# Attention and two MoE layers in one kernel: three units of the first stage transposed by VectorE and moved by GpSimd's queue, and the fourth chunk's bias written a group at a time

## The chip, the cores and the metric

One core of a Trainium2 chip runs one program. The metric is device time in microseconds (us), the median of several executions. The engines are TensorE (PE in the profile, its weight loads PEld), VectorE (DVE), ScalarE (ACT), GpSimd (POOL) and SyncE (SP, which here only issues transfers). A transfer is issued by a queue (SP's, GpSimd's, ScalarE's) and carried by the same 16 DMA engines.

## The reference

Attention with a bias that depends on the distance of the two positions, then two feed-forward layers (their weights are float64, the rest float32), for 4 sequences of 576 tokens, 8 heads of 64:

```python
x = (np.log1p(np.abs(rel)) / psi_i)[..., None]
h = np.maximum(x @ w1 + b1, 0.0)            # 32 hidden values
bias = h @ w2                               # one per head
scores = scale * np.matmul(q, k.transpose(0, 1, 3, 2)) + bias.transpose(2, 0, 1)[None]
attn = softmax(scores); out = np.matmul(attn, v)
x = attention output as 2304 tokens x 512
y = (sigmoid(x @ w_gate) * (x @ w_val)) @ w_out          # 512 -> 1536 -> 512
h = y @ w_in                                             # 512 -> 2048
out = (h * np.clip(h + 3, 0, 6) / 6) @ w_out2            # 2048 -> 512
```

## The kernel before, in words

The 576 query positions are cut into five chunks (`QC`, line 25), four of 128 and one of 64. The work goes in stages: a first stage computes the attention of chunk 0, and then block k (k = 0 to 4, `block`, line 833) computes the feed-forward layers of chunk k in 68 steps of 12 matmuls (`moe_step`, line 592; `product`, line 565), with the attention of chunk k+1 put in between. TensorE executes its instructions in the order in which they are written. In the first stage all engines but GpSimd keep the written order (`manual_schedule`, line 648), in block 0 TensorE and SP, later TensorE alone; the rest is ordered by the tile framework's scheduler.

**The first stage** (lines 645 to 703) handles 16 units. A unit is one sequence and a pair of heads, 128 queries by 2 x 576 keys. After the bias of the first chunk and of four groups of the second, the loop over n (line 679) has these parts in iteration n:

- `att_load` (281): SP's loads of unit n+3. The pools hold 6 buffers of k and 7 of v.
- `att_exp` (330), ScalarE: the exponentials of unit n.
- `att_min` (315), VectorE: unit n+1's scores plus bias, with their minimum (of the negated scores). It frees the PSUM buffers into which `att_qk` writes next.
- `att_tr` (351): unit n-1's nine 128x128 transposes on TensorE, in three parts, each copied by ScalarE from PSUM into `pT`.
- `att_norm` (339), VectorE: unit n divided by its sums.
- `att_av` (390), TensorE: the products with V of unit n-2, and `att_x` (410): their high half on ScalarE (424) and low half on VectorE (425).
- `att_qk` (299), TensorE: unit n+2's products of q and k. They need both PSUM buffers of `s1`, so unit n+1's minimum first.
- `w_part` (509), VectorE: one sixth of the conversion of one of the first two weight blocks from packed doubles into a high and a low half; block 0 on iterations 4 to 9, block 1 on 10 to 15. The sixth part also issues the store of the converted block on SP's queue (533).

From block 0 on, weights are loaded with `w_load` (495), converted with `w_split` (536, first use of each block) and, from block 1 on, read back converted.

**Later chunks.** Chunk 1 is transposed as above. Chunks 2 to 4 are handled by pairs of units (`chunk_pairs`, 765): `pair_qk` (428), `pair_soft` (473), whose `att_turn` (368) lets VectorE transpose each 32x32 block (line 373), and `pair_turn` (378), which moves the blocks to their partitions with 16 transfers (line 383), on GpSimd's queue, for chunks 2 and 3 half of them on SP's. The products with V (`pair_av`, 486) follow `lag` steps after the start of the pair.

**The bias.** A group G is 16 query positions. `bias_hidden` (136) makes the hidden values of a quarter of a group, on ScalarE or VectorE; `bias_mm` (153) multiplies them with w2 on TensorE; for chunks 1 to 3 the bias is symmetric, and `bias_out2` (177) writes two groups at once, the right part on ScalarE, the mirrored left part on VectorE, into a tile, and issues two transfers to DRAM. With `apart` it takes each group's result from a buffer of `m1` (four one-bank PSUM buffers, line 77, which the matmuls of the steps, of the transposes, of `pair_qk`'s tails and of the products with V use too) rather than from `s1` (two buffers of two banks, line 76, which hold the scores). `cv_t` (95) holds a constant per partition, which replaces a term for the quarters that VectorE makes.

**Order and due times.** `block_events` (809) gives each piece of attention work a due step; `block` carries out what is due before each step's 12 matmuls. For block 1 (k = 1): chunk 2's bias from step 2, pairs of chunk 2 at 21 + 5.11 i, chunk 3's bias at (line 820)

```python
ev += chunk_bias(3, 23.2 + 1.5 * d, d / 2)
```

with d = 46/9 = 5.11 steps. In block 3 the last chunk's four pairs start 18.8 steps apart, from 0.5, and the products with V come 10 steps after a start, the last at step 67 (line 828). Steps 24 to 35 and 46 to 53 of a block are the output products, in which an open sum stays in one buffer of `m1` for three or two steps.

## Time and profile before

| | us |
|---|---|
| median of 3 runs | 1108.26 |
| lowest and highest of them | 1106.01, 1110.21 |
| the profiled execution | 1106.79 |
| its span in the profile | 1105.0 |

| engine | share of the span in which it is busy |
|---|---|
| TensorE matmuls | 99% |
| TensorE weight loads (beside them) | 80% |
| VectorE | 60% |
| ScalarE | 47% |
| GpSimd | 12% |

The span reaches from the first to the last instruction of the profiled execution; 1.79 us of its time lie around it. Busy time of TensorE is modelled at its end, as its matmuls overlap; whether it stands still is read from its waits. The profile's lines give an instruction as line, engine, operation, output <- inputs by the names in the program. "Idle before" is the engine's time without work just ahead of an instruction, with what ended it. The chain of waits follows back, from the last instruction, what each one waited for.

### The profile page before, as it was taken

To read this page: it belongs to the slowest core of one execution; us is meant where nothing else is said; L and a number is where in the kernel's file an instruction comes from. 1 tells how busy PE (TensorE), PEld (TensorE's weight loads), DVE (VectorE), ACT (ScalarE), POOL (GpSimd) and SP (SyncE) were. 2 spreads that over 40 slices of the span, in tenths; PEclk is the share of its full clock that TensorE was granted. 3 is DMA by queue.
4 is the path that set the end of the run, shared out by engine and by line. 5 is a ranking of instruction groups with operands and counts; after the bars stand their busy time and mean duration, and the time that the engine had idled before them with its cause. 6 is when DMAs were issued, how large, how long until landed. Compare 5 with 4: busy or idle time off the path is not lost.

```text
span 1105.0 us, 19878 instructions
## 1 busy us (share of the span) xinstructions
PE 1094.5 (99%) x7142; PEld 884.0 (80%) x7142; DVE 668.0 (60%) x1529; ACT 524.7 (47%) x1052; POOL 129.7 (12%) x248
## 2 busy tenths in 40 slices
PE   8999999999999999999999999999999999999998
PEld 4777777777777788777888878788788787879998
DVE  7999998898963456897725654656252417052232
ACT  7887686798863433565414342534032214121132
POOL 1000000000010002112221111111430202031000
PEclk9999999999999999999999999999999999999999
DMA  6958999999987688999988888798896978778997
GB/s 228 369 182 296 373 396 373 386 322 375 384 292 233 219 264 281 283 311 294 342 296 249 292 245 278 250 281 244 283 274 239 266 247 255 227 215 310 363 365 270
DMA packets 118769, 321.97 MB, mean 291 GB/s; under 512 B 21008, under 2 KB 29712, under 8 KB 118672
## 3 DMA queue, kind: packets, MB, share of 16 engines
q1 hardware_dynamic: 108000, 297.15, 79.0%
q0 software_dynamic: 9152, 23.21, 7.5%
q8 instruction: 57, 0.93, 0.3%
q10 hardware_dynamic: 1520, 0.35, 0.1%
q14 instruction: 40, 0.33, 0.1%
HBM read 245.09 MB, written 51.37 MB: 268 GB/s over the span
## 4 chain that ended last, share of the span: by engine, by line
PE 80%; DVE 7%; DMA 5%; ACT 4%; issue 3%; POOL 1%; ACTq 0%; DVEq 0%; POOLq 0%
PE ps L574 63%; PE ps L404 7%; PE ps L309 3%; PE ps L446 3%; PE ps L360 2%; DMA pT<-t 2%; PE ps L162 1%; PE ps L170 1%; DVE cm L546 1%; DMA wsp<-wp 1%; DVE cm L549 1%; DVE wp L555 1%; POOL outT L635 1%; ACT cm L544 1%; DVE s L324 1%
## 5 line engine op out<-in xcount | busy, mean ns | idle before, releaser
L574 PE MATMUL ps<-xyh,wp 128*128 128x512 f32 (+1 forms) x1600 | 468.1, 372 | 0.3
L574 PEld LDWEIGHTS ps<-xyh,wp 128*128 128x128 f32 x1600 | 290.5, 189 | 61.3 <-issue 4.9
L574 PE MATMUL ps<-gh,wp 128*128 128x512 f32 (+1 forms) x1120 | 330.2, 373 | 0.0
L574 PE MATMUL ps<-xyl,wp 128*128 128x512 f32 (+1 forms) x800 | 295.6, 370 | 0.4 <-DVE xyl L587 0.3
L574 PEld LDWEIGHTS ps<-gh,wp 128*128 128x128 f32 x1120 | 203.5, 189 | 37.8 <-issue 3.6
L574 PE MATMUL ps<-gl,wp 128*128 128x512 f32 (+1 forms) x560 | 206.9, 369 | 0.0
L574 PEld LDWEIGHTS ps<-xyl,wp 128*128 128x128 f32 x800 | 151.1, 189 | 24.6 <-DVE xyl L587 0.8
L383 POOL DMA_DIRECT2D pT<-t x192 | 94.3, 499 | 504.1 <-DVE t L373 136.3
L583 ACT ACTIVATE gh<-tmp 128x512 fp32r<-128x512 f32 (+1 forms) x140 | 82.2, 588 | 145.9 <-DVE tmp L605 103.3
L334 ACT ACTIVATE s<-s,m 128x576 f32<-128x576 f32 x144 | 110.4, 768 | 20.1 <-DVE m L468 14.4
L574 PEld LDWEIGHTS ps<-gl,wp 128*128 128x128 f32 x560 | 105.8, 189 | 16.8 <-DVE gl L585 0.6
L585 DVE TENSOR_TENSOR gl<-tmp,gh 128x512 fp32r<-128x512 f32 (+1 forms) x140 | 88.6, 634 | 47.3 <-ACT gh L583 46.4
L605 DVE SCALAR_TENSOR_TENSOR tmp<-tmp,ps 128x512 f32<-128x512 f32 (+1 forms) x60 | 37.8, 630 | 94.1 <-PE ps L574 92.7
L404 PEld LDWEIGHTS ps<-pT,vt 128*64 128x64 f32 x1600 | 79.4, 137 | 18.1 <-issue 12.6
L404 PE MATMUL ps<-pT,vt 128*64 128x128 f32 (+1 forms) x1600 | 92.4, 266 | 1.5 <-DMA pT<-t 0.9
L611 DVE SCALAR_TENSOR_TENSOR tmp<-tmp,ps 128x512 f32<-128x512 f32 (+1 forms) x80 | 50.0, 628 | 57.1 <-ACT tmp L610 55.5
L424 ACT ACTIVATE xyh<-ps 128x128 fp32r<-128x128 f32 (+1 forms) x52 | 16.5, 317 | 107.3 <-PE ps L404 107.1
L610 ACT ACTIVATE tmp<-ps 128x512 f32<-128x512 f32 (+1 forms) x80 | 43.9, 549 | 41.9 <-PE ps L574 40.4
L425 DVE TENSOR_TENSOR xyl<-ps,xyh 128x128 fp32r<-128x128 f32 (+1 forms) x52 | 17.7, 341 | 72.4 <-ACT xyh L424 72.1
L601 ACT ACTIVATE tmp<-ps 128x512 f32<-128x512 f32 (+1 forms) x60 | 33.1, 552 | 56.9 <-PE ps L574 56.9
L635 POOL DMA_DIRECT2D outT<-acc x40 | 27.7, 736 | 262.3 <-DVE acc L626 245.1
L147 ACT ACTIVATE z<-tz_t,zc_t,sc_t 128x576 f32<-128x576 f32 (+7 forms) x70 | 49.7, 766 | 13.2 <-PE ps L162 11.3
(73 smaller groups left out, 1096.5 us busy)
## 6 DMA issues: line engine op xcount, KB each, us to landing
wp<-wsp SPq DMA_DIRECT2D x272, 512.0 KB, 5.2
wd<-wpack SPq DMA_DIRECT2D x68, 512.0 KB, 6.7
wsp<-wp SPq DMA_DIRECT2D x68, 512.0 KB, 6.2
vt<-vd SPq DMA_DIRECT2D x80, 320.0 KB, 5.2
kt<-kd SPq DMA_DIRECT2D x80, 288.0 KB, 5.1
pT<-t POOLq DMA_DIRECT2D x192, 72.0 KB, 5.3
pT<-t SPq DMA_DIRECT2D x128, 72.0 KB, 5.0
bm<-biasD SPq DMA_DIRECT2D x15, 576.0 KB, 5.9
```

What stands on the lines that cost most here:

```text
L147: nc.scalar.activation(out=z, in_=x, func=AF.Relu, scale=sc_t[:, t:t + 1], bias=b1c)
L309: nc.tensor.matmul(out=ps[h][n * a:n * a + n, j, 0:NI], lhsT=qt[r, b + a, 0:n], rhs=kt[r, NI * j:NI * j + NI], start=True, stop=True, tile ...
L334: nc.scalar.activation(out=s[:, h], in_=s[:, h], func=AF.Exp, scale=-1.0, bias=d["m"][:, h:h + 1], accum_out=r[:, h:h + 1],)
L383: (nc.sync if p[0][0] < 4 and i > 1 else nc.gpsimd).dma_start(out=pt[32 * q:32 * q + 32, i].rearrange("j u t i -> j (u t i)"), in_=t[32 * ...
L404: nc.tensor.matmul(out=po[64 * h:64 * h + 64, n * a:n * a + n], lhsT=vt[:, v], rhs=pt[:, m * a:m * a + m, k, :], start=(t == 0), stop=(t = ...
L574: nc.tensor.matmul(out=ps[:, 0:nt], lhsT=w[:, c, :], rhs=x[:, 0:nt], start=(first and c == 0 and i == 0), stop=(last and c == 3 and i == 2),)
L583: nc.scalar.activation(out=hi[:, 0:nt], in_=src, func=AF.Copy, scale=scale)
L585: nc.vector.tensor_tensor(out=lo[:, 0:nt], in0=src, in1=hi[:, 0:nt].bitcast(F32), op=ALU.subtract)
L605: nc.vector.scalar_tensor_tensor(out=th, in0=th, scalar=1.0, in1=ps, op0=ALU.add, op1=ALU.mult)
L610: nc.scalar.activation(out=t, in_=ps, func=AF.Relu, bias=3.0)
L611: nc.vector.scalar_tensor_tensor(out=t, in0=t, scalar=6.0, in1=ps, op0=ALU.min, op1=ALU.mult)
L635: q.dma_start(out=out[2 * ih + x, o, :, :, lo - ih * NI:hi - ih * NI], in_=av[:, 2 * x:2 * x + 2, lo - i0:hi - i0],)
```

## The change

In the first stage three of the 16 units (numbers 2, 6 and 10) are no longer transposed by TensorE. VectorE transposes the 32x32 blocks of such a unit in one instruction, right after its scaling, into a tile with one buffer, and GpSimd's queue moves the blocks with 16 transfers of 36 KB into another tile, with two buffers. The products with V of such a unit come in iteration n+5 instead of n+2, ahead of the usual ones of that iteration. v has ten buffers instead of seven. The parts of the two weight conversions fall on other iterations (`CONV`). The two second-chunk groups that are written apart get a constant of their own, `cv1_t`, with one more quarter's product.

In the second block the fourth chunk's bias is made by groups: each group's hidden values half a pair's distance ahead of a pair's start, its products and its writing (`bias_out1`, SP's queue) just before that start, in one-bank buffers. In the fourth block the products with V of the last chunk's first three pairs come 11.5 steps after a start instead of 10.

```diff
--- before.py
+++ after.py
@@ -93,6 +93,7 @@
     sc_t = const.tile([128, S // 4], F32, name="sc_t")
     zc_t = const.tile([128, 3], F32, name="zc_t")
     cv_t = const.tile([128, 1], F32, name="cv_t")
+    cv1_t = const.tile([128, 1], F32, name="cv1_t")
     wm_t = const.tile([128, 1], F32, name="wm_t")
     w2b_t = const.tile([128, 32], F32, name="w2b_t")
     id_t = const.tile([128, 128], F32, name="id_t")
@@ -112,12 +113,13 @@
     nc.vector.tensor_scalar(out=sc_t, in0=sc_t, scalar1=zc_t[:, 0:1], scalar2=None, op0=ALU.mult)
     nc.vector.tensor_scalar(out=zc_t[:, 2:3], in0=b1c, scalar1=-1.0, scalar2=None, op0=ALU.mult)
     ps = mm_ps()
-    for g in (2, 3):
+    for g in (1, 2, 3):
         nc.tensor.matmul(
             out=ps[32 * g:32 * g + 32, 0:2], lhsT=w2b_t, rhs=zc_t[:, 0:2], start=True, stop=True,
             tile_position=(0, 32 * g),
         )
     nc.vector.tensor_scalar(out=cv_t[64:128], in0=ps[64:128, 1:2], scalar1=D ** 0.5, scalar2=None, op0=ALU.mult)
+    cps = ps
 
 
 
@@ -184,12 +186,12 @@
         if apart:
             for x, p in enumerate((ps, bo_q.pop(G + 1))):
                 nc.scalar.activation(
-                    out=bo[:, x, left:SU], in_=p[:, 0:right + 1], func=AF.Identity, scale=D ** 0.5, bias=cv_t
+                    out=bo[:, x, left:SU], in_=p[:, 0:right + 1], func=AF.Identity, scale=D ** 0.5, bias=cv1_t
                 )
             for x, p in enumerate((ps, p)):
                 nc.vector.tensor_scalar(
                     out=bo[:, x, 0:left], in0=p[:, left:0:-1],
-                    scalar1=D ** 0.5, scalar2=cv_t, op0=ALU.mult, op1=ALU.add,
+                    scalar1=D ** 0.5, scalar2=cv1_t, op0=ALU.mult, op1=ALU.add,
                 )
         else:
             nc.scalar.activation(
@@ -212,6 +214,26 @@
             (nc.gpsimd if c == 1 else nc.sync).dma_start(
                 out=rows[16 * x:16 * x + 16], in_=bo[:, x, 0:SU],
             )
+
+    def bias_out1(G):
+
+        ps = bo_q.pop(G)
+        c, x = 16 * G // NQ, G % 2
+        i0 = 16 * (G - x) - QC[c][0]
+        left, right, _ = reach(G)
+        if x == 0:
+            bo_t[1] = A["bo"].tile([128, 2, SU + 1], F32, name="bo")
+        bo = bo_t[1][:, x]
+        nc.scalar.activation(
+            out=bo[:, left:SU], in_=ps[:, 0:right + 1], func=AF.Identity, scale=D ** 0.5, bias=cv_t
+        )
+        nc.vector.tensor_scalar(
+            out=bo[:, 0:left], in0=ps[:, left:0:-1],
+            scalar1=D ** 0.5, scalar2=cv_t, op0=ALU.mult, op1=ALU.add,
+        )
+        at = NQ - 32 - i0
+        rows = biasD[c].rearrange("(h r w) -> r h w", h=H, w=SW)[i0 + 16 * x:i0 + 16 * x + 16, :, at:at + SU]
+        nc.sync.dma_start(out=rows, in_=bo[:, 0:SU])
 
     def bias_out(G, x=0, last=True):
 
@@ -365,6 +387,20 @@
             in_=ps[:, 0:3 * NQ].rearrange("p (t n) -> p t n", t=3), func=AF.Copy,
         )
 
+    def unit_turn(u):
+
+        t = A["t"].tile([128, 4, 9, 32], F32, name="t")
+        pt = st[u]["pt"] = A["pu"].tile([128, 4, 9, 32], F32, name="pT")
+        nc.vector.transpose(
+            out=t, in_=st[u]["s"].rearrange("p h j -> p (h j)").rearrange("p (t q j) -> p q t j", q=4, j=32)
+        )
+        for i in range(4):
+            for q in range(4):
+                nc.gpsimd.dma_start(
+                    out=pt[32 * q:32 * q + 32, i].rearrange("j t i -> j (t i)"),
+                    in_=t[32 * i:32 * i + 32, q].rearrange("j t i -> j (t i)"),
+                )
+
     def att_turn(p, x):
 
         u = p[x]
@@ -392,7 +428,7 @@
         n = QC[c][1]
         d = st[u]
         vts, pt = kv_q.pop(u)[1], d["pt"]
-        if c < 2:
+        if c < 2 and u not in TURNED:
             pt = pt.rearrange("j t (p i) -> j p t i", i=32)
         m = n // 32
         po = d["po"] = o_ps()
@@ -642,8 +678,11 @@
     us = units[0]
     NL = len(us)
     NG0, NG1 = QC[0][1] // 16, 2
+    TURN = (2, 6, 10)
+    TURNED = [us[n] for n in TURN]
+    CONV = (5, 7, 9, 11, 13, 14, 15, 15, 15, 16, 16, 17)
     with ExitStack() as lead:
-        for name, bufs in (("pt", 2), ("s", 3), ("k", 6), ("v", 7), ("bo", 3), ("wf", 2), ("cv", 2)):
+        for name, bufs in (("pt", 2), ("s", 3), ("k", 6), ("v", 10), ("t", 1), ("pu", 2), ("bo", 3), ("wf", 2), ("cv", 2)):
             A[name] = lead.enter_context(tc.tile_pool(name=name + "l", bufs=bufs))
         lead.enter_context(tc.manual_schedule(engines={ET.PE, ET.Activation, ET.DVE, ET.SP}))
         load_rows(us[0], False)
@@ -670,6 +709,8 @@
         for G in range(NG0 + NG1, NG0 + NG1 + 2):
             for g in range(4):
                 bias_hidden(G, g, 1)
+        nc.vector.tensor_scalar(out=cv1_t, in0=cv_t, scalar1=1.0, scalar2=None, op0=ALU.mult)
+        nc.vector.tensor_scalar(out=cv1_t[32:64], in0=cps[32:64, 1:2], scalar1=D ** 0.5, scalar2=None, op0=ALU.mult)
         att_qk(us[0])
         for G in range(NG0 + NG1, NG0 + NG1 + 2):
             bias_mm(G, True)
@@ -685,18 +726,22 @@
                 att_exp(us[n])
             if n + 1 < NL:
                 att_min(us[n + 1])
-            if 1 <= n <= NL:
+            if 1 <= n <= NL and n - 1 not in TURN:
                 for part in range(3):
                     att_tr(us[n - 1], part, mm_ps)
             if n < NL:
                 att_norm(us[n])
-            if n >= 2:
-                att_av(us[n - 2], mm_ps)
-                att_x(us[n - 2])
+            if n in TURN:
+                unit_turn(us[n])
+            for m in (n - 5, n - 2):
+                if m >= 0 and (m in TURN) == (m == n - 5):
+                    att_av(us[m], mm_ps)
+                    att_x(us[m])
             if n + 2 < NL:
                 att_qk(us[n + 2])
-            if 4 <= n < 16:
-                w_part((n - 4) // 6, (n - 4) % 6)
+            for part in range(12):
+                if CONV[part] == n:
+                    w_part(part // 6, part % 6)
             if n == NL - 4:
                 gate = issued[0]
             if n == NL:
@@ -817,7 +862,10 @@
             d = (last - 21.0) / 9
             ev += chunk_bias(2, 2.0, 1.5)
             ev += chunk_pairs(2, 21.0, d, 2 * d, last)
-            ev += chunk_bias(3, 23.2 + 1.5 * d, d / 2)
+            for g in range(8):
+                a = 21.0 + d * (g + 1)
+                ev.append((a - d / 2, lambda G=24 + g: [bias_hidden(G, t) for t in range(4)]))
+                ev.append((a - 0.005, lambda G=24 + g: (bias_mm(G, True), bias_out1(G))))
         elif k == 2:
             d = (last - 9.5 - 0.5) / 7
             n4 = 2 * S - 4 - 4 * 16 * 8
@@ -825,7 +873,7 @@
             ev += chunk_pairs(3, 0.5, d, d, last)
             ev += chunk_bias(4, d + 2.7, d)
         elif k == 3:
-            ev += chunk_pairs(4, 0.5, (last - 10.5) / 3, 10.0, last)
+            ev += chunk_pairs(4, 0.5, (last - 10.5) / 3, 11.5, last)
         return [e[::2] for e in sorted((e[0], n, e[1]) for n, e in enumerate(ev))]
 
     held = []
```

## Rows read from the trace of the kernel before

**Rows 1.** The page: busy time by engine; chain that ended last, by engine.

```profile
PE 1094.5 (99%) x7142; PEld 884.0 (80%) x7142; DVE 668.0 (60%) x1529; ACT 524.7 (47%) x1052; POOL 129.7 (12%) x248
...
PE 80%; DVE 7%; DMA 5%; ACT 4%; issue 3%; POOL 1%; ACTq 0%; DVEq 0%; POOLq 0%
```

**Rows 2.** What TensorE waited for, whole kernel: us in total, times, longest us.

```profile
PE ps L404 <- DMA pT<-t: 0.9, 1, 0.9
...
PE ps L360 <- DVE s L347: 0.4, 1, 0.4
```

**Rows 3.** Chain of waits in the first stage: start us, us, what.

```profile
43.09 1.17 PE ps L309 x8
44.26 1.14 PE ps L360 x9
45.40 1.24 PE ps L404 x20
...
81.50 1.17 PE ps L360 x9
...
88.48 11.63 PE ps L574 x50
```

**Rows 4.** Busy us by stretch, first stage: length, engines (instructions), PEclk, DMA share, GB/s.

```profile
35.93:50.12 14.19, 14.19 (x151) 10.91 (x149) 12.24 (x39) 11.82 (x32) 0.00 (x0) 1.00 1.04 389
...
sum 42.65, PE 42.63 PEld 32.71 DVE 39.51 ACT 35.46 POOL 0.00; mean PE 14.21 PEld 10.90 DVE 13.17 ACT 11.82 POOL 0.00
```

**Rows 5.** VectorE's timeline, first stage: start us, us, instruction, idle before it.

```profile
37.20 0.76 DVE L324 CUSTOM_DVE_ANT_0 s<-ps,bm 128x576 f32<-128x576 f32 x1 [0.55 <-PE ps L309]
...
40.75 0.76 DVE L324 CUSTOM_DVE_ANT_0 s<-ps,bm 128x576 f32<-128x576 f32 x1 [0.55 <-PE ps L309]
...
42.11 0.16 DVE L341 TENSOR_SCALAR r<-r 128x2 f32<-128x2 f32 x1
...
43.45 0.29 DVE L425 TENSOR_TENSOR xyl<-ps,xyh 128x128 fp32r<-128x128 f32 x1
43.66 0.43 DVE L518 TENSOR_SCALAR cm<-wd 128x512 f32<-128x512 f32 x1
...
47.84 0.76 DVE L324 CUSTOM_DVE_ANT_0 s<-ps,bm 128x576 f32<-128x576 f32 x1 [0.22 <-PE ps L309]
...
50.75 0.68 DVE L522 SCALAR_TENSOR_TENSOR cm<-wd,cm 128x512 uint32<-128x512 uint32 x1
51.39 0.76 DVE L324 CUSTOM_DVE_ANT_0 s<-ps,bm 128x576 f32<-128x576 f32 x1
```

**Rows 6.** VectorE's timeline, second block, a transposition.

```profile
410.06 1.38 DVE L373 STREAM_TRANSPOSE t<-s 128x1152 f32<-128x1152 f32 x1
```

**Rows 7.** GpSimd's timeline, its transfers of transposed pairs.

```profile
412.07 3.95 POOL L383 DMA_DIRECT2D pT<-t  x8 [72.57 <-issue]
...
638.17 4.03 POOL L383 DMA_DIRECT2D pT<-t  x8 [20.65 <-DMA wp<-wsp]
...
869.00 4.03 POOL L383 DMA_DIRECT2D pT<-t  x8 [45.87 <-DVE t L373]
...
877.17 2.44 POOL L383 DMA_DIRECT2D pT<-t  x5 [1.38 <-DMA pT<-t]
```

**Rows 8.** DMA issues, 20 to 36 us: KB each, median us to landing.

```profile
bm<-bo SPq DMA_DIRECT2D x2, 36.0 KB, 2.3
```

**Rows 9.** DMA issues by line, 868.5 to 886 us.

```profile
pT<-t POOLq DMA_DIRECT2D x16, 72.0 KB, 6.0
```

**Rows 10.** Tile pT, 412 to 424 us: landing of its transfers.

```profile
DMA to landing us min/median/max: 3.2/3.8/4.5
```

**Rows 11.** SP's timeline, first stage: issue of the first block's store.

```profile
62.10 0.33 SPq L533 DMA_DIRECT2D wsp<-wp  x1
```

**Rows 12.** VectorE's timeline, first block's start and third block.

```profile
88.47 1.29 DVE L555 TENSOR_TENSOR wp<-cm,wp 128x512 fp32r<-128x512 f32 x2
...
638.12 2.03 DVE L149 TENSOR_SCALAR z<-tz_t,sc_t,zc_t 128x576 f32<-128x576 f32 x4
```

## The prediction

> **What bounds the kernel now.** I read the page's busy line and its chain first: TensorE is busy for 1094.5 of 1105.0 us, and the chain that ended last is 80% TensorE [rows 1]. Then the list of what TensorE waited for: nine waits in the whole kernel, none above 1.1 us; two that matter below are in [rows 2]. So no stage has idle time to win back. The kernel gets shorter only by work that leaves TensorE or by one of these waits, and longer by every new one.
>
> In the first stage (to 84 us) the chain goes in iterations of one unit: products of q and k 1.17 us, nine transposes 1.14, products with V 1.24, together 3.55 [rows 3]. The busy times of its steady part show that VectorE is nearly as full: 39.5 of 42.65 us, TensorE 42.63, at a granted clock of 1.00, the 2.4 GHz level [rows 4]. VectorE's timeline gives one iteration: the minimum 1.36 us (40.75 to 42.11), the scaling 1.34 (to 43.45), the low half of an output 0.21 (to 43.66). That is 2.91, and then one part of a weight conversion, 0.43 long or 0.64 to the next start (50.75 to 51.39). An iteration with the long part, 47.84 to 51.39, takes 3.55 us and has no gap [rows 5]. VectorE's room is thus 0.64 us in an iteration without a part, and nothing in one with a long part.
>
> **The change, part by part.**
>
> *Off TensorE and ScalarE:* three times nine transposes, 3 x 1.14 = 3.4 us of TensorE; and nine copies on ScalarE, which has room (35.5 of 42.65 us [rows 4]) and so gives nothing.
>
> *Onto VectorE:* three transpositions of 128x1152; one of that shape takes 1.38 us [rows 6]. The parts of the conversions move to make room: one on each of iterations 5, 7, 9, 11, 13 and 14, six on 15 to 17.
>
> *What VectorE then can do, iteration by iteration.* Before, the minimum of unit 4 starts at 37.20 after 0.55 us of waiting [rows 5]. The first transposition, 1.38, comes ahead of it: 0.83 later, 38.0. Iterations 3 to 5 take 2.91, 2.70 (no products with V, so no low half) and 2.91 + 0.43: the minimum of unit 7 starts at 46.95, before at 47.84. Iterations 6 to 9 take 2.91 + 1.38, 2.91 + 0.21 + 0.43, 2.70, and 2.91 + 0.64: 14.1 us, where the kernel before took 4 x 3.55 = 14.2 and TensorE alone would need 14.2 - 1.14 = 13.1. Iterations 10 to 13 come to 14.1 again. So unit 15's minimum starts at 75.15, some 1.05 us earlier than before (47.84 + 8 x 3.55 = 76.2), and not 3.4. VectorE sets the pace, and TensorE stands for a few tenths at a time.
>
> *The tail gives that back.* With its last q·k product done at about 75.3, TensorE has two groups of transposes and two products with V ahead of unit 15's transposes, and now also unit 10's product, which is five behind: 2 x 1.14 + 3 x 1.24 = 6.0, and some 0.3 for the scaling of unit 14: 81.6, against 81.50 [rows 3]. I put the first stage at **0.0**; its ends are -2.6 (the second rival) and late data (the first).
>
> *Will the data be there?* Behind each transposition sixteen transfers of 36 KB go out from GpSimd's queue, in which nothing stands in that stretch (0.00 us busy [rows 4]). Eight issues take 3.95 us [rows 7], sixteen 7.9 to 8.2. No row shows such a transfer from this queue. Its landing lies between 2.3 us, a 36 KB transfer from SP's queue [rows 8], and 6.0, this pattern with 72 KB in a full stretch [rows 9]; there the queue also stood for earlier landings, so that sixteen issues took from 869.00 to 879.61, 10.6 us [rows 7]. From the end of a transposition to the last landing that makes 7.9 + 2.3 = 10.2 to 10.6 + 6.0 = 16.6 us. I take 12.0: 8.2 and the 3.8 of a 72 KB stretch in which the queue never stood [rows 10], because half the bytes weigh against the fuller DMA here. The first to wait is VectorE itself, as the transposed tile has one buffer. The first transposition ends at about 37.7 (the low half that waited for nothing but its product, 0.29, then 0.55 of idle, move behind it), the second is due at 46.95 + 2.70 = 49.6, so 11.9 us are there: just in time, no cost, no margin.
>
> *SP's queue.* The store of the first converted block stood in it until 62.10 [rows 11], waiting for the sixth part, with the loads of units 13 to 15 behind it. It now follows all the loads, and V has ten buffers for seven: loads only get earlier. They also fill a stretch that was nearly free of transfers while unit 6's transfers run, which speaks for the first rival.
>
> *The six late parts* (3 x 0.43 + 3 x 0.64 = 3.2 us) delay VectorE's conversion of the third weight block. It is ready at 88.47 + 0.7 = 89.2 [rows 12]. The 50 products from 88.48 on [rows 3] are two that end the first step and four steps of 2.8 us, so the third step starts at 91.7. VectorE's three transpositions and these parts are 1 to 2.5 us there: no cost, up to 0.5.
>
> *Start.* One more product of two columns, two VectorE instructions of one column, long before anything waits for them: no cost, up to 0.2.
>
> *Fourth chunk's bias a group at a time* (second block). The same products and the same eight transfers; eight narrower evictions of each kind for four wide ones. No wait of TensorE lies there, so nothing is won. But the results now take a buffer of the pool of four: at steps 32 and 47 an open sum holds one, and the pair's second tail needs the one of the products with V just ahead. If VectorE is in a transposition then, TensorE stands 1.38 us at most; the bias products between give it more than that time. No cost, up to 1.4 at each of two places.
>
> *Last chunk's products with V 1.5 steps later.* One wait was there, 0.9 us [rows 2]; a step of 2.8 us is now between. **-0.9**, with 0 as the other end if the transfers are later too.
>
> Sum: 0.0 + 0.0 - 0.9. The profiled execution took 1106.79 us, 1.79 more than its span; so 1105.9. The median of the three runs shown is 1.47 above that execution: **1107.4 us**.
>
> **A rule weighed.** While VectorE ran four scalings, 2.03 us from 638.12 [rows 12], eight issues of GpSimd took 4.03 us, against 3.95 without [rows 7]. *The Trainium skill, "SBUF — State Buffer", section "Who interferes with whom", says that a VectorE instruction in a two-port mode, into which scalings can go, and GpSimd shut each other out for the whole instruction; by that the eight issues would have taken up to 2 us longer, and this row does not show it.* I keep 3.95; the other outcome is the third rival.
>
> **Rivals.**
>
> *Data late (slower).* With 16.6 us, the second transposition stands 16.6 - 11.9 = 4.7 us on VectorE, and behind it every minimum for which TensorE's next q·k product waits. The third has 14.1 - 1.4 = 12.7 us, so 0 to 3.9 more. It decides from about 12 us on. For it: transfers at 1.04 of the DMA's share in 35.93 to 50.12 [rows 4], and earlier loads. Against: half the bytes. Middle price 6: 1113.4 us. Chance 0.18.
>
> *VectorE keeps up (faster).* By totals VectorE needs 39.5 + 4.1 - 3.2 = 40.4 us in the steady part and TensorE 42.6 - 3.4 = 39.2, so at least 1.2 of the 3.4 is lost; with the wait of 0.4 before unit 15's transposes [rows 2] gone, -2.6. For it: these totals; against: the order inside each four iterations. 1107.4 - 2.6 = 1104.8. Chance 0.14.
>
> *Issues stop while VectorE scales.* Two scalings are at most 1.3 us of each 3.55 (the 1.34 above). Sixteen issues would take 7.9 x 3.55 / 2.25 = 12.5, the data is there after 16.3, 4.4 late, then 3.6: 1107.4 + 8 = 1115.4. Chance 0.04.
>
> *Buffers of the second block* decide: 1.4 twice, 1110.2. Chance 0.06.
>
> **How the numbers follow.** My forecast has 0.58; its own range, with the spread of the three runs (1106.0 to 1110.2), is 1105.5 to 1109.5. Half a per cent, about what a measurement of this kernel can tell from no change, is 5.5 us: below 1102.7 or above 1113.8. The first needs the second rival and luck: 0.04. The second needs the dearer half of the late data, or the third rival: 0.11. Between them 0.85. The range 1104.0 to 1113.0 takes in the second and fourth rival and the cheaper half of the first; it leaves out some 0.04 below and 0.13 above.
>
> **What would show it.** Right: 13 groups of nine transposes for 16 in the first stage; VectorE without gaps from 37 to 75 us and TensorE waiting there for a minimum or a scaling; unit 15's transposes still near 81.5; no wait for the three units' transfers, and none at the last chunk. Wrong: products with V (line 404) or VectorE's transposition waiting for a transfer (late data); unit 15's transposes before 79.5 (VectorE keeps up); waits of TensorE in the second block (buffers).

## The result, and the profile after

The changed kernel takes 1117.06 us (median of 6 runs, 1115.99 to 1121.29), the kernel before 1106.82 in the same series: a ratio of 1.0093, 95% interval 1.0078 to 1.0107 (the ratios here and below are taken from the executions, not from the two medians, and so are not always their quotient). It is slower, and outside the range. The span of the profiled execution is 1114.8 us, 9.8 more than before.

The page of the changed kernel, busy time by engine and the chain that ended last, against [rows 1]:

```profile
PE 1095.8 (98%) x7117; PEld 882.8 (79%) x7117; DVE 672.3 (60%) x1538; ACT 522.9 (47%) x1047; POOL 154.8 (14%) x296
...
PE 89%; DMA 4%; DVE 3%; ACT 1%; issue 1%; POOL 1%; SPq 0%; ACTq 0%; DVEq 0%
```

TensorE is busy as long as before (1095.8 against 1094.5 us). The 9.8 us are therefore mostly waits. The chain does not say which: transfers of `pT` have 2% of it before and after. TensorE's list of waits does (us in total, times, longest), against [rows 2]:

```profile
PE ps L440 <- DMA pT<-t: 6.7, 2, 3.5
PE ps L610 <- DVE wp L591: 1.5, 3, 0.7
```

The first line is new, and it alone is 6.7 us. TensorE's timeline (start us, us, instruction, idle before it) has its two places, the products with V of units 2 and 6, each in one row with those of an ordinary unit, hence x40. The third row, with unit 10's, waits for nothing. The last four rows I use further below:

```profile
54.22 2.40 PE L440 MATMUL ps<-pT,vt 128*64 128x128 f32 x40 [3.52 <-DMA pT<-t]
...
72.07 3.79 PE L440 MATMUL ps<-pT,vt 128*64 128x128 f32 x40 [3.22 <-DMA pT<-t]
...
87.14 2.40 PE L440 MATMUL ps<-pT,vt 128*64 128x128 f32 x40
...
107.92 1.50 PE L164 MATMUL ps<-z,w2b_t 128*32 128x384 f32 x16
...
137.29 0.73 PE L610 MATMUL ps<-xyh,wp 128*128 128x512 f32 x2 [0.53 <-DVE wp L591]
...
154.87 0.50 PE L610 MATMUL ps<-xyh,wp 128*128 128x512 f32 x1 [0.51 <-ACT wp L590]
...
360.61 1.28 PE L164 MATMUL ps<-z,w2b_t 128*32 128x320 f32 x16
```

VectorE stands for the same transfers, since its transposed tile has one buffer:

```profile
36.58 1.38 DVE L394 STREAM_TRANSPOSE t<-s 128x1152 f32<-128x1152 f32 x1
...
54.20 1.38 DVE L394 STREAM_TRANSPOSE t<-s 128x1152 f32<-128x1152 f32 x1 [4.32 <-DMA pT<-t]
...
72.06 1.38 DVE L394 STREAM_TRANSPOSE t<-s 128x1152 f32<-128x1152 f32 x1 [4.02 <-DMA pT<-t]
```

GpSimd's queue shows why, in the same columns (six of its eight rows):

```profile
38.27 4.11 POOL L399 DMA_DIRECT2D pT<-t  x8 [8.72 <-DVE xyl L461]
43.61 0.50 POOL L399 DMA_DIRECT2D pT<-t  x1 [1.24 <-DMA pT<-t]
44.68 3.85 POOL L399 DMA_DIRECT2D pT<-t  x7 [0.57 <-DMA pT<-t]
55.87 4.31 POOL L399 DMA_DIRECT2D pT<-t  x8 [7.34 <-DVE xyl L461]
...
74.00 2.45 POOL L399 DMA_DIRECT2D pT<-t  x5 [7.62 <-PE ps L440]
76.63 5.67 POOL L399 DMA_DIRECT2D pT<-t  x11 [0.18 <-issue]
```

The first eight issues go out in 4.11 us, against 3.95 in [rows 7]. Then the queue stands until one of them has landed (1.24 us), and issues the rest by 48.53. From the end of the first transposition (37.96) to the start of the second (54.20, which waits for the last landing) are 16.2 us; after the second (55.58 to 72.06) 16.5. The view of the tile `pT` has the landings of single transfers for the first, second and third unit, in us:

```profile
DMA to landing us min/median/max: 5.1/5.7/7.2
...
DMA to landing us min/median/max: 5.4/6.1/6.7
...
DMA to landing us min/median/max: 1.7/1.7/3.6
```

Busy time by stretch (columns as in [rows 4], with the granted clock and the DMA's share near the end):

```profile
54.00:64.00 10.00, 9.48 (x94) 7.13 (x94) 9.59 (x29) 6.08 (x16) 6.52 (x12) 1.00 1.06 362
64.00:72.00 8.00, 4.85 (x49) 3.41 (x45) 3.83 (x11) 4.74 (x13) 1.98 (x5) 1.00 1.00 339
72.00:80.00 8.00, 7.93 (x66) 6.29 (x66) 7.73 (x22) 4.23 (x12) 5.82 (x12) 0.79 0.22 59
...
73.00:76.00 3.00, 3.00 (x30) 2.67 (x28) 2.93 (x10) 0.38 (x2) 2.00 (x5) 0.50 0.11 27
```

The first two units' transfers run beside SP's loads at a share of 1.00 to 1.06. The first unit would have met a full DMA in the kernel before too (1.04 in [rows 4]). The second would not; this is the kernel before there:

```profile
50.00:64.00 14.00, 14.00 (x150) 10.78 (x148) 13.50 (x41) 11.82 (x32) 0.00 (x0) 1.00 0.50 174
```

Up to 64 us the changed kernel has twice that: the loads are earlier, as the diff lets them be. The third unit's run at 0.22, and one lands in 1.7 instead of 5.7 or 6.1 us. The last row of the changed kernel is the clock: behind the wait of 3.22 us TensorE ran at 0.50, the 1.2 GHz level, so that the same 40 products took 3.79 us (72.07) instead of 2.40 (54.22). Waits of 6.7 us and 1.4 us of slower products make 8.1, about what the first stage loses.

To see where the rest went, I use two instructions that stand behind the same work in every kernel, but for the transposes that left TensorE: block 0's first product of a bias group (behind its first 60 weight products), at 107.92 in TensorE's timeline above, and block 1's, at 360.61. In the kernel before they start at 100.05 and 350.06. Between them the rows at 137.29 and 154.87 are two of four new waits for converted weights.

The first stage ends 7.87 us later, block 0 takes 252.69 us instead of 250.01, block 1 (to block 2's first bias product, 286.95 against 286.08) 0.87 more: 11.4. Of these 1.6 come back later.

### The profile page after: what moved, and what is told of

Read it like the earlier page. It is cut to its first block, busy times and chain, and to the rows that moved or that the text cites. A ratio compares the mean times of both kernels' runs of the same rounds, so it can differ in the third digit from the quotient of the medians.

```text
span 1114.8 us, 19919 instructions
## 1 busy us (share of the span) xinstructions
PE 1095.8 (98%) x7117; PEld 882.8 (79%) x7117; DVE 672.3 (60%) x1538; ACT 522.9 (47%) x1047; POOL 154.8 (14%) x296
## 4 chain that ended last, share of the span: by engine, by line
PE 89%; DMA 4%; DVE 3%; ACT 1%; issue 1%; POOL 1%; SPq 0%; ACTq 0%; DVEq 0%
PE ps L610 72%; PE ps L440 7%; PE ps L482 2%; DMA pT<-t 2%; PE ps L331 2%; PE ps L382 2%; PE ps L164 2%; PE ps L172 1%; DMA wd<-wpack 1%; PE ps L488 1%; POOL pT L399 1%; ACT z L149 0%; DVE s L346 0%; DVE s L504 0%; DVE s L369 0%
## 5 line engine op out<-in xcount | busy, mean ns | idle before, releaser
L460 ACT ACTIVATE xyh<-ps 128x128 fp32r<-128x128 f32 (+1 forms) x52 | 16.5, 318 | 114.9 <-PE ps L440 114.9
L409 DVE STREAM_TRANSPOSE t<-s 128x1152 f32<-128x1152 f32 x40 | 54.3, 1369 | 0.5
```

Of the source, the lines that this page charges most:

```text
L409: nc.vector.transpose(out=tn_q[0][:, :, x], in_=st[u]["s"].rearrange("p h j -> p (h j)").rearrange("p (t q j) -> p q t j", q=4, j=32),)
```

## The experiments

One table first; each row is explained below. "First stage" is the start of block 0's first bias product, "block 0" the time from there to block 1's.

| kernel | first stage, us | block 0, us | median, of before, us | ratio, 95% interval |
|---|---|---|---|---|
| before | 100.05 | 250.01 | | |
| changed | 107.92 | 252.69 | 1117.06, 1106.82 | 1.0093, 1.0078 to 1.0107 |
| e1, stage alone | 107.99 | 253.12 | 1117.21, 1108.18 | 1.0091, 1.0069 to 1.0112 |
| e2, rest alone | 100.25 | 250.25 | 1107.04, 1108.18 | 0.9993, 0.9982 to 1.0004 |
| e3, late parts alone | 100.30 | 252.78 | 1109.69, 1108.18 | 1.0010, 0.9995 to 1.0025 |
| e5, three k | 105.53 | 252.04 | 1114.04, 1108.18 | 1.0062, 1.0047 to 1.0078 |
| e4, seven behind | 109.99 | 250.63 | 1116.99, 1107.60 | 1.0078, 1.0053 to 1.0103 |
| e7, and early parts | 103.09 | 252.87 | 1112.68, 1107.60 | 1.0051, 1.0031 to 1.0070 |
| e6, and ScalarE scales | 111.81 | 255.25 | 1122.26, 1107.60 | 1.0123, 1.0098 to 1.0149 |
| e8, lag alone | 100.25 | 251.42 | 1106.75, 1107.60 | 0.9992, 0.9979 to 1.0005 |
| e10, seven behind, clean | 100.98 | 253.13 | 1109.85, 1107.35 | 1.0037, 1.0014 to 1.0060 |
| e11, and early parts | 103.87 | 249.87 | 1110.69, 1107.35 | 1.0025, 1.0010 to 1.0040 |
| e12, one unit | 102.20 | 252.92 | 1111.65, 1107.35 | 1.0037, 1.0024 to 1.0051 |
| e13, fifth buffer | 101.52 | 256.97 | 1114.16, 1107.95 | 1.0060, 1.0039 to 1.0080 |

The theory after the result was late data: transfers beside a full DMA take 16 us. The rivals were VectorE's pace, GpSimd's issuing, and the late conversion parts.

**e1 and e2: which half?** e1 keeps the edits of the first stage and takes the others back, e2 the reverse (no unit turned, parts on 4 to 15, seven buffers for V).

```diff
-            for g in range(8):
...
+            ev += chunk_bias(3, 23.2 + 1.5 * d, d / 2)
-            ev += chunk_pairs(4, 0.5, (last - 10.5) / 3, 11.5, last)
+            ev += chunk_pairs(4, 0.5, (last - 10.5) / 3, 10.0, last)
```

```diff
-    TURN = (2, 6, 10)
+    TURN = ()
-    CONV = (5, 7, 9, 11, 13, 14, 15, 15, 15, 16, 16, 17)
+    CONV = tuple(range(4, 16))
```

> Only the first-stage part of the change is in; the bias of the fourth chunk and the last chunk's lag are as before. If the first stage is the whole loss, the span grows by what the trace of the changed kernel shows up to the start of block 1 (about +10.5 us: some 7.5 in the first stage and 2.7 in block 0), so about 1117.5 us. If the bias by groups is part of it, about 1116 us, less than 1 us under the changed kernel.

> Only the other two parts: the fourth chunk's bias a group at a time and the last chunk's products with V 11.5 steps after a start. From the trace of the changed kernel: +0.9 us in block 1 (of which 0.6 is the narrower bias products: 8 of 0.84 to 1.04 us for 4 of 1.53 to 1.85), -1.2 in block 3. So 0.3 us faster than before, no difference that the runs can tell. A rival by which these parts carry the loss says +2 us or more.

Both came as expected: the first stage's edits have the whole loss, the bias by groups and the later products nothing that can be told from no change. Block 1 is 286.94 us in e1 too, which has the bias by pairs, so its 0.87 does not come from the groups. In e8, whose block 1 is the program of before, it is 286.59: 0.5 us come without any edit to that block, and the rest I leave open.

**e3: the late parts alone**, in the kernel before (`CONV` as in the change; the extra constant at the start stays in, too).

```diff
-                w_part((n - 4) // 6, (n - 4) % 6)
+            for part in range(12):
+                if CONV[part] == n:
+                    w_part(part // 6, part % 6)
```

> The kernel before with one thing changed: the parts of the two weight conversions on the late iterations. Theory: the six parts at the end of the stage and the later stores delay VectorE's next conversions and the raw weights' loads, and TensorE then waits for converted weights in block 0: waits on the conversion of 1 to 2 us in all, span +1 to +2.7. Rival: the 2.7 us of block 0 come from the late stage as such (loads of block 0 in another state); then this kernel waits for no converted weights and takes the time of the one before, within 0.5 us.

What TensorE waited for in e3 (none of it in the kernel before):

```profile
PE ps L610 <- DVE wp L591: 1.5, 3, 0.7
...
PE ps L610 <- ACT wp L590: 0.9, 2, 0.5
```

Block 0 is 252.78 us long, as in the changed kernel. The timed ratio, 1.0010, cannot tell this from nothing or from 2.7 us, so the block's length, from one trace, has to say it; e10, e11 and e13 come back to it.

**e5: the loads later**, with the transfers as they are.

```diff
-        for name, bufs in (... ("k", 6), ("v", 10), ...):
+        for name, bufs in (... ("k", 3), ("v", 10), ...):
```

> The changed kernel with three buffers of k for six, nothing else: SP's loads then cannot run more than three units ahead, so they follow TensorE's pace instead of filling the DMA engines. Theory (late data through full DMA engines): the landing of the three units' transfers falls from 5.6 us to about 2 to 3.5, the sixteen issues no longer stand and take 8 to 8.5 us, the waits of 3.5 and 3.2 us for them go, and the stage ends 5 to 7 us earlier: about 1110 us. Rival 1 (VectorE is too slow for the three transpositions anyway): the waits for the transfers go, but waits for minima and scalings take their place, about 1115. Rival 2 (GpSimd issues slowly beside VectorE's scalings): sixteen issues still take over 10 us and the waits stay, about 1117. If the fewer buffers make TensorE wait for k itself, its waits on loads of k will show it.

TensorE's timeline at the products of units 2, 6 and 10:

```profile
54.83 3.45 PE L440 MATMUL ps<-pT,vt 128*64 128x128 f32 x40 [3.42 <-DMA pT<-t]
...
69.82 2.40 PE L440 MATMUL ps<-pT,vt 128*64 128x128 f32 x40
...
84.72 2.40 PE L440 MATMUL ps<-pT,vt 128*64 128x128 f32 x40 [0.60 <-DMA pT<-t]
```

The first unit's transfers still meet a full DMA (1.04 and 1.06 in 36 to 54 us) and are as late. The second's run at 0.82 (54 to 64 us), and its data are there. The third's, which met a nearly idle DMA in the changed kernel, now run at 0.79 (71 to 84 us) and are 0.60 us late. GpSimd's timeline for them:

```profile
56.48 8.57 POOL L399 DMA_DIRECT2D pT<-t  x16 [8.21 <-DVE xyl L461]
```

Sixteen issues in one go take 8.57 us while VectorE scales beside them: GpSimd is not slow, and the rival falls. With 4.0 us of waits for `pT` left of 6.7, and a new one of 1.5 us for k, the first stage is 2.4 us shorter. The time missed: 1110 was expected of late data and 1115 of VectorE's pace, and it lies between, as the edit spared only one unit of three.

**e4 and e7: seven units behind**, so that the transfers have 7 us more; two buffers for the transposed tile, three for `pT`, twelve for V. e7 has the parts on 4 to 15 as well.

```diff
-            for m in (n - 5, n - 2):
-                if m >= 0 and (m in TURN) == (m == n - 5):
+            for m in (n - 7, n - 2):
+                if m >= 0 and (m in TURN) == (m == n - 7):
...
```

> The changed kernel with the products with V of units 2, 6 and 10 seven units behind instead of five, two buffers for the transposed tile instead of one, three for what the transfers fill, twelve for V. The same transfers go out at the same places; only the time that they may take grows by two iterations, 7 us. Late data (my theory): the 16 us from transposition to landing stay, but neither VectorE (4.32 and 4.02 us before) nor TensorE (3.52 and 3.22) waits for them, the clock stays at its upper level, and the first bias product of the first block starts 0 to 1.5 us after that of the kernel before (100.12 us) instead of 7.9. The late conversion parts still cost 2.2 to 2.7 and the groups 0.6 to 0.9 us, the last chunk gives back 1.2: 2 to 4 us over the kernel before, about 1110 us. Rival, VectorE too slow: the waits are only another sign of its pace; the marker stays 5 us or more late and the time near 1114. Rival, GpSimd's queue too slow: the second set of transfers starts later than its transposition ends, and VectorE waits at the third.

> The run with the products seven units behind, and the conversion parts back on iterations 4 to 15, one each. If the late parts are what the first block loses, its four waits for converted weights (0.3 to 0.7 us each) are gone and it takes 250.0 us from its first bias product to the end again instead of 252.7; the first stage pays for it, as VectorE's four iterations come to about 15.1 instead of 14.1 us: 1 to 2.5 us later. Together about the same as the run seven behind, within 1 us: near 1110. Rival, the late parts cost nothing: the first block stays as long and the run is 1 to 2.5 us slower than the one seven behind.

The times missed. In e4 the waits for the three units are gone (58.92 is unit 2's product), but a greater one has come, in the first step of block 0:

```profile
58.92 2.40 PE L440 MATMUL ps<-pT,vt 128*64 128x128 f32 x40
...
98.63 0.79 PE L610 MATMUL ps<-xyh,wp 128*128 128x512 f32 x1 [5.51 <-ACT wp L590]
```

Behind it stands ScalarE's conversion, which waited 3.8 us for a load of packed weights, and that load was late in SP's queue:

```profile
81.18 8.43 SPq L569 DMA_DIRECT2D wsp<-wp  x2
89.66 8.65 SPq L536 DMA_DIRECT2D wd<-wpack  x5
```

In the changed kernel four loads of packed weights are issued from 59.71 on, ahead of the stores of both converted blocks, the first of which is at 87.23:

```profile
59.71 3.67 SPq L536 DMA_DIRECT2D wd<-wpack  x4
87.23 0.33 SPq L569 DMA_DIRECT2D wsp<-wp  x1
```

In e4 they stand behind both stores, at 89.66, and in e7 behind them too. With fewer buffers, in e10, the old order is back. I read it so that the buffers I had added moved the memory of these loads onto buffers still in use; no run shows this reading by itself. So e4, e6 and e7 each changed two things, and say little about the first stage. e4 does show the clock again, granted 0.50 after 5.51 us of waiting:

```profile
98.00:102.00 4.00, 3.37 (x8) 2.39 (x9) 3.78 (x7) 1.81 (x3) 0.00 (x0) 0.50 0.74 233
```

**e6: ScalarE scales the turned units**, their transposition an iteration later, otherwise as e4.

```diff
-            if u[0] == 1:
+            if u[0] == 1 or u in TURNED:
                 nc.scalar.activation(out=s[:, h], in_=s[:, h], func=AF.Identity, scale=r[:, h:h + 1])
```

> The run with the products seven units behind, and the scaling of the three turned units on ScalarE instead of VectorE, their transposition one iteration later, behind the next unit's minimum. If VectorE sets the pace of the first stage once the data are no longer late, the stage becomes about 1.3 us shorter for each turned unit that still sits inside it, so 2 to 3.5 us in all against the run seven behind, and 1107 us comes out. Rival, TensorE's own work or ScalarE sets it: within 0.5 us of the run seven behind.

It missed: 5 us slower than e4. The scaling delays the copies and high halves behind it on ScalarE, and VectorE stands for them at each of the three units, as here:

```profile
36.94 0.29 DVE L461 TENSOR_TENSOR xyl<-ps,xyh 128x128 fp32r<-128x128 f32 x1 [1.73 <-ACT xyh L460]
```

That covers only the first stage, 1.8 us longer than e4's. Block 0 is 4.6 us longer, and why stays open.

**e8: the lag alone**, 11.5 steps for 10 in the kernel before.

```diff
-            ev += chunk_pairs(4, 0.5, (last - 10.5) / 3, 10.0, last)
+            ev += chunk_pairs(4, 0.5, (last - 10.5) / 3, 11.5, last)
```

> The kernel before with the last chunk's products with V 1.5 steps later and nothing else. By the trace of the changed kernel the fourth block becomes 1.2 us shorter: 1105.7 us, 0.999 of the kernel before. Rival, the wait was hidden by something next to it: 1106.9, no difference.

The difference is 0.85 us by the medians, with an interval on both sides of none. The wait of [rows 2] is gone in e8's trace, as in the changed kernel's. But it is gone in e1's too, which keeps the 10 steps.

**e10 and e11: seven units behind with the old order of SP's queue**; e11 has the parts on 4 to 15.

```diff
-        for name, bufs in (... ("v", 10), ("t", 1), ("pu", 2), ("bo", 3), ...):
+        for name, bufs in (... ("v", 10), ("t", 2), ("pu", 2), ("bo", 2), ...):
-            for m in (n - 5, n - 2):
-                if m >= 0 and (m in TURN) == (m == n - 5):
+            for m in (n - 7, n - 2):
+                if m >= 0 and (m in TURN) == (m == n - 7):
```

> Seven behind once more, with so much less memory (two buffers for what the transfers fill, ten for V, two for the bias's results) that SP's queue has the order of the changed kernel again: the loads of the first block's packed weights ahead of the stores, not behind. In the run seven behind they stood behind, and one wait of 5.5 us on a weight in the first step, with the fall of the clock after it, hid what was gained. Late data (my theory): no wait for the three units' transfers, and the first bias product of the first block at about 102.5 us, 2.5 over the kernel before (0.3 of it the start, 1.1 unit 10's product at the very end, 1.1 VectorE's pace), where the changed kernel has 107.9; the late parts' cost in the first block stays, 1 to 2.7: 1109 to 1112 us. Rival, VectorE too slow whatever the data do: marker at 105 or later, near 1115.

> The same with the conversion parts on iterations 4 to 15, one each, as in the kernel before. If the late parts delay the third block of weights and so the first block, it takes 250.0 to 251.5 us from its first bias product to the first of the next, where the changed kernel took 252.7; the marker itself comes 0 to 1 us later than in the run before this, as VectorE has more to do inside the stage. About 1 us faster than that run: 1108 to 1111. Rival, the late parts cost nothing: 0 to 1 us slower.

e10 settles the first stage (TensorE's timeline; units 2 and 6 with an ordinary one, unit 15's transposes, the two markers):

```profile
57.99 2.40 PE L440 MATMUL ps<-pT,vt 128*64 128x128 f32 x40
...
73.02 2.40 PE L440 MATMUL ps<-pT,vt 128*64 128x128 f32 x40
...
81.91 1.18 PE L382 MATMUL ps<-id_t,s 128*128 128x128 f32 x9 [0.44 <-DVE s L369]
...
100.98 1.50 PE L164 MATMUL ps<-z,w2b_t 128*32 128x384 f32 x16
...
354.11 1.28 PE L164 MATMUL ps<-z,w2b_t 128*32 128x320 f32 x16
```

The first two units' transfers, beside a DMA share of 1.05 to 1.07, land as late as before (5.8 us in the middle), but nothing waits for any unit's. The first stage ends at 100.98, 6.94 us earlier than in the changed kernel and 0.93 later than in the kernel before, 1.5 better than I expected; the medians, of two series, are 7.2 us apart, the ratios 0.6%, some 6 us. So late data is the cause of the first stage's loss, and VectorE's pace (expected by that rival at 105 or later) is not. That pace explains why nothing is won either: 27 transposes, 3.4 us by [rows 3], have left TensorE, and the stage is still no shorter. Block 0 keeps its 253.13 us.

e11 does what was expected of block 0: 249.87 us. Its first stage pays 2.89 us, where 0 to 1 was expected, so the run is no faster than e10; two waits for k, 1.96 us together, are part of that (the longer one here, and the markers):

```profile
40.77 1.24 PE L331 MATMUL ps<-kt,qt 64*128 64x288 f32 x8 [1.34 <-DMA kt<-kd]
...
103.87 1.50 PE L164 MATMUL ps<-z,w2b_t 128*32 128x384 f32 x16
...
353.74 1.28 PE L164 MATMUL ps<-z,w2b_t 128*32 128x320 f32 x16
```

With the late parts, and the loads of packed weights ahead of the second store, block 0 takes 252.69, 253.12, 252.78, 252.04 and 253.13 us (changed, e1, e3, e5, e10); with the parts on 4 to 15 it takes 250.01, 250.25, 251.42 and 249.87 (before, e2, e8, e11). That is 2.4 us between the means. Each is one trace, and before and e8, which are the same program there, are 1.4 apart; the pairs that differ in little but the parts, before and e3, e10 and e11, are 2.8 and 3.3 apart. e4 (late parts, 250.63) and e7 (early parts, 252.87), whose loads stand behind both stores, go the other way, so the place of the parts does not decide alone.

**e12: one unit turned.**

```diff
-    TURN = (2, 6, 10)
+    TURN = (10,)
-    CONV = (5, 7, 9, 11, 13, 14, 15, 15, 15, 16, 16, 17)
+    CONV = (4, 5, 6, 7, 8, 9, 12, 13, 14, 15, 16, 16)
-        for name, bufs in (... ("v", 10), ("t", 1), ("pu", 2), ...):
+        for name, bufs in (... ("v", 8), ("t", 1), ("pu", 1), ...):
...
```

> One turned unit only, the tenth's place (10), five behind, when SP's loads thin out; conversion parts on iterations 4 to 16 with none on 10 and 11; the fourth chunk's bias by pairs as before; last chunk 1.5 steps later. One group of nine transposes (1.14 us) goes, VectorE gets 1.38 less what the two free iterations give (0.64 each), the last chunk gives 1.2 by the trace. If the loss is late data and VectorE's fullness, both are small here: 1106 to 1108, no difference or 1 us faster. Rival, each turned unit costs 2 to 3 us whatever surrounds it: 1109 to 1110.

It missed, because SP's loads had not thinned out; the time is nearer to the rival's. The store of the first block is early again and the loads stand behind it, as in the kernel before, so that the DMA's share is 1.00 in 64 to 72 us. The one unit's data are late as well:

```profile
81.29 2.40 PE L440 MATMUL ps<-pT,vt 128*64 128x128 f32 x40 [1.80 <-DMA pT<-t]
```

From the end of its transposition (66.59) to that product are 14.7 us. In the changed kernel the same unit's transfers met a DMA nearly idle and cost no wait. Block 0 is long here too; the last parts are on 15 and 16. The rival's fixed price, 2 to 3 us for each unit, does not hold all the same: e10's three units lengthen the first stage by 0.93 us.

**e13: a fifth buffer for the packed weights**, in e10, to see how the late parts cost 2.4 us.

```diff
-    for name, bufs in (("pt", 2), ("wf", 4), ("cv", 2)):
+    for name, bufs in (("pt", 2), ("wf", 5), ("cv", 2)):
```

> The run seven behind with the right order of SP's queue, and a fifth buffer for the packed weights of the first block, so that the fifth load no longer waits until VectorE has read the third block's. If the late parts cost the first block its 2.7 us through that load (a chain of load, conversion, product that keeps the delay), the block comes back to 250 to 251.5 us from its first bias product to the first of the next, and the run to 1107 to 1108 us, no difference from the kernel before. Rival, VectorE and ScalarE themselves fall behind there: the block stays at 252.5 to 253.2 and the run at 1110.

My theory fell, and the rival's range was passed as well. The fifth load is issued by 66.1 us instead of at 88.48, and yet block 0 takes 256.97 us. TensorE waits for conversions in the same stretch, 29 to 46 us behind the first marker (29 to 56 in e10), and longer, and the clock falls behind two of these waits (the last row is a stretch, with 0.53 granted in it):

```profile
145.71 0.50 PE L610 MATMUL ps<-xyh,wp 128*128 128x512 f32 x1 [1.33 <-ACT wp L590]
...
147.45 1.15 PE L610 MATMUL ps<-xyh,wp 128*128 128x512 f32 x2 [1.01 <-DVE wp L591]
...
147.40:150.50 3.10, 3.05 (x7) 2.43 (x8) 3.06 (x6) 1.97 (x4) 0.00 (x0) 0.53 1.06 388
```

The order of ScalarE's and VectorE's instructions in block 0 also differs between the kernels with early and with late parts, and again in e13. That the delay lies in this order is argued, not shown: no kernel here had the late parts with the order of before. How the late parts cost block 0 its time stays open.

No version beat the kernel before: the fastest, e8, cannot be told from it.

## Why the prediction was wrong

- **Off TensorE**: right, 13 groups of nine transposes for 16.
- **What VectorE can do**: nearly right. The minima of units 4, 7, 11 and 15 were put at 38.0, 46.95, 61.05 and 75.15. In e10, where no data are late, they start at 37.72, 46.83, 61.60 and 76.62; five rows of its VectorE timeline:

```profile
46.83 0.76 DVE L346 CUSTOM_DVE_ANT_0 s<-ps,bm 128x576 f32<-128x576 f32 x1 [0.21 <-PE ps L331]
...
60.75 0.29 DVE L461 TENSOR_TENSOR xyl<-ps,xyh 128x128 fp32r<-128x128 f32 x1 [0.80 <-ACT xyh L460]
...
61.60 0.76 DVE L346 CUSTOM_DVE_ANT_0 s<-ps,bm 128x576 f32<-128x576 f32 x1
...
75.78 0.29 DVE L461 TENSOR_TENSOR xyl<-ps,xyh 128x128 fp32r<-128x128 f32 x1 [0.80 <-ACT xyh L460]
...
76.62 0.76 DVE L346 CUSTOM_DVE_ANT_0 s<-ps,bm 128x576 f32<-128x576 f32 x1 [0.21 <-PE ps L331]
```

The two groups of four iterations took 14.8 and 15.0 us, not 14.1. In each, two products with V follow one another, and the low half of the second waits 0.80 us for ScalarE's high half. I had counted its 0.21 us of work and not this wait.
- **The tail gives that back**: right in the main, but the agreement of the start is luck. Unit 15's transposes were put at 81.6 and start at 81.91 in e10. Unit 15's minimum came 1.5 us later than I had it, and one product of 1.24 us that my sum has ahead of the transposes, unit 10's, stands behind them in e10, which is seven behind and not five. The first stage without late data is 0.9 us longer; I had 0.0.
- **Will the data be there?** This step failed. I took 12.0 us from transposition to last landing, against 11.9 available; it was 16.2 and 16.5, at the upper bound of 16.6. I had the landing from a stretch in which the queue never stood (3.8 us, [rows 10]; the DMA's share was 0.79 there), because half the bytes would weigh against the fuller DMA. They did not: 36 KB took 5.7 and 6.1 us, like the 72 KB of [rows 9] in a full stretch (1.03). The kernel before has more such stretches that my rows leave out: its 72 KB transfers of `pT` took 5.1 us at 1.01 (462 to 480 us) and 7.3 at 0.97 (510 to 530). And the two of [rows 8], 2.3 us, were issued in a half empty one (0.52 in 20 to 22 us). So landing followed how full the DMA was more than the bytes of the transfer. With it came the standing queue of [rows 7]: 10.3 us for sixteen issues, not 8.2.
- **SP's queue**: the direction was right, the weight was not. The earlier loads, which I named as speaking for the first rival, put the second unit's transfers beside a share of 1.06.
- **The six late parts**, "no cost, up to 0.5": wrong, 2.4 us in block 0 by the traces. I had looked only at the third weight block, due at 91.7, and TensorE indeed does not wait there. In the changed kernel it waits from 137.29 on, 29 us behind the first marker.
- **Start** and **the bias by groups**, no cost: right. The first marker is at 100.25 in e2, with the edit at the start, and in e8, without it. **The last chunk**, -0.9: the wait is gone, but as e1 shows it can go without the edit; the timing cannot tell.
- **Rivals.** Data late had the mechanism, the place and nearly the price: 4.7 us for the second transposition (measured 4.32), 0 to 3.9 for the third (4.02), 6 in all (6.94). Its 1113.4 us is short by the late parts and that 0.9. I gave it 0.18 for a sum that stood at 12.0 against 11.9 with bounds of 10.2 and 16.6; the middle of these, 13.4, was already late. "Issues stop while VectorE scales" had 12.5 us for sixteen issues and is refuted by the 8.57 of e5. "VectorE keeps up" is refuted by e10, whose first stage is 0.9 us longer and not 2.6 shorter. "Buffers of the second block" did not come: with these edits and the later products alone, e2 cannot be told from the kernel before, and no wait of TensorE in the changed kernel's second block is above 0.4 us.

*The Trainium skill, "SBUF — State Buffer", section "Who interferes with whom", speaks of VectorE and GpSimd shutting each other out; in e5 sixteen issues of GpSimd took 8.57 us while VectorE scaled beside them, against 7.9 for twice the eight of [rows 7], so by these rows about 0.7 us (an estimate) of the 16 between a transposition and its last landing could come from it.*

## What to carry to other kernels

Where a landing differs by 4 us between a full and a nearly idle DMA, price it by how full the DMA is when it will run, with the change's own effect on the loads, not by a row of like size from an emptier stretch. Where time needed and time available agree within a tenth and the bounds are 6 us apart, late is the likely case: give the data more time, as e10 did, before judging the idea. And buffers added can change the order of transfers elsewhere, as in e4: look whether later transfers kept their place in their queue.

## What the runs showed of the hardware

- A 36 KB transfer from tile to tile, issued from GpSimd's queue, lands in 1.7 us with the DMA nearly idle (share 0.22) and in 5.7 to 6.1 beside loads that fill it (1.00 to 1.06). In between the share alone does not order the rows: in e5 the middle landing is 3.5 us at 0.77 (56 to 67 us) and 5.7 at 0.79 (71 to 84).
- A wait of 3.22 us brought TensorE to the 1.2 GHz level for the stretch behind it (granted 0.50 from 73 to 76 us), in the middle of a busy kernel; one of 3.52 us in the same run did not (x40 in 2.40 us), one of 3.42 us in e5 did (3.45 us). In e13 two waits of 1.33 and 1.01 us, with two matmuls between them, did too (0.53 from 147.4 to 150.5 us). *The Trainium skill, "TensorE: Matmul & The Clock Gate", section "Part 1: The HAM clock gate (the "warmup" mystery)", says that the clock is halved after idleness; these rows agree in that, and show that waits of nearly one length can go either way and that two shorter ones close together did the same.*
